# Slots in two rooms, fixed PSUM bank pairs and a first block split ahead, in a kernel of attention and two expert layers

## The chip, the cores and the metric

The kernel runs on one core of a Trainium2 chip. The metric is the device time of one execution in microseconds (us); smaller is better. Work is done by the engines PE (TensorE, matrix products), ACT (ScalarE), DVE (VectorE) and POOL (GpSimd); SP (SyncE) issues nearly all DMA transfers. A step of an engine waits on semaphores for what it needs, and each engine, SP too, works through its own list in order. SBUF is the on-chip memory, PSUM the banks that PE writes its sums into.

## The reference, cut to what matters

```python
def _attn_ref(q, k, v):                         # each 8 x 8 x 576 x 64
    q_s = np.exp(q - np.max(q, axis=-1, keepdims=True))
    q_s = q_s / (np.sum(q_s, axis=-1, keepdims=True) + 1e-09)
    k_s = np.exp(k - np.max(k, axis=2, keepdims=True))
    k_s = k_s / (np.sum(k_s, axis=2, keepdims=True) + 1e-09)
    kv = np.einsum('bhsd,bhse->bhde', k_s, v)
    return np.einsum('bhsd,bhde->bhse', q_s, kv)

def _moe_ref(x, w_in, w_out):                   # x 4608 x 512, w_in 512 x 2048, w_out 2048 x 512
    h = x @ w_in
    return (h * (1.0 / (1.0 + np.exp(-1.702 * h)))) @ w_out

def _moe2_ref(x, w_in, w_out):                  # the same sizes
    h = x @ w_in
    g = np.where(h >= 1, h, np.where(h <= -1, 0.0, (h + 1) ** 2 / 4.0))
    return g @ w_out
```

The output is `_moe2_ref` of `_moe_ref` of the attention's tokens, 4608 x 512 in fp32. The weights come as 64-bit floats and are converted on the chip.

## The kernel before, in words

There are four large products, one after the other, and each is a stage of the program:

1. The **first stage** is attention and the first GEMM (L403 to L405), in nine token blocks of 512 (blocks 0 to 8). A block has 16 column groups `m`, worked off in eight pairs. A pair fills a two-bank PSUM tile `hps` (two such tiles), ACT takes its sigmoid into a tile `sg` (L411, three buffers), DVE multiplies (L412), and SP stores the result as `g0_<block>_<pair>` in DRAM (L413). Attention's work for block j stands in the steps of block j-1, so the last block, 8, has nothing beside its own GEMM. The tokens of a block lie in `xh` and `xl`, two sets that take turns.
2. **pass_out(0)** (gemm L637) multiplies by the first w_out.
3. **pass_in** (gemm L754) multiplies by the second w_in and applies the piecewise function (`finish`, L772 to L774, with the store L777 of `g1`).
4. **pass_out(1)** is pass_out again, with the second w_out, and with the outputs transposed on PE (`turn`).

Every fp32 operand is split in two: ACT copies it rounded to `hi` (L103), DVE subtracts to get `lo` (L104), and each product is three: hi·hi, lo·hi and hi·lo. The last three stages also replace eight block products by seven, in the order PROD = 1, 7, 6, 2, 5, 4, 3 over the quadrants "11", "12", "22" and "21" of a token block, with sums of tiles on DVE (`tt`, L107). There are five token blocks. In a pass_out, a **step** is one (block, p, i) with i from 0 to 3: 12 matmuls that need one split tile. Steps 0 to 3 are p = 1, steps 4 to 7 are p = 7, and so on. Step s is split three steps ahead (LA = 3), into slots that are taken in rotation from R_AT: hi and lo of step s are entries 2s and 2s+1.

**Slots.** After the first stage, its SBUF pools are closed and 27 slots `s0` to `s26` of 4 KB per partition are opened. s0 to s15 hold the loaded tiles (G_AT), and s16 and up are shared out by R_AT (splits of a pass_out), O_AT (its results), E_AT (results of pass_in) and W_AT (conversion of weights in pass_in). Waits between users of a slot go tile by tile.

**PSUM** pools are opened and closed by stage: `hps` and attention's, then z and zx of each pass. `widen` (L535) issues matmuls whose sums nobody uses, two at the head of each pass_out and four at the head of pass_in.

**Order.** The program is laid down in Python order, and a scheduler may move an instruction of an engine ahead of others. SP's DMAs use eight semaphores DMAHW0 to DMAHW7 in turn, so each waits for the one eight before it. The loads of pass_out(0)'s first block stand behind the last `g0` store, at L572 (`Quadrants.load`). Those of pass_out(1)'s first block stand as hooks in the last group of pass_in, at L566.

Of the kernel before, what the change touches and what calls it, by code (L numbers as in the profile page):

```python
# [8 lines left out]
FP32 = mybir.dt.float32  # L9
# [9 lines left out]
def kernel(  # L19
# [11 lines left out]
    nc = tc.nc  # L31
# [27 lines left out]
    half = const.tile([P, 96], FP32, name="half")[:, :1]  # L59

# [124 lines left out]

    with ExitStack() as st0:
        vpool = st0.enter_context(tc.tile_pool(name="va", bufs=1))
        kpool = st0.enter_context(tc.tile_pool(name="k", bufs=3))
        kfpool = st0.enter_context(tc.tile_pool(name="kf", bufs=4))
        qpool = st0.enter_context(tc.tile_pool(name="q", bufs=4))  # L190
        qtpool = st0.enter_context(tc.tile_pool(name="qt", bufs=1))
        sm1 = st0.enter_context(tc.tile_pool(name="sm1", bufs=1))
        sm = st0.enter_context(tc.tile_pool(name="sm", bufs=2))
        xpool = st0.enter_context(tc.tile_pool(name="x", bufs=1))
        sgp = st0.enter_context(tc.tile_pool(name="sg", bufs=3))
        ps_h = st0.enter_context(tc.tile_pool(name="ps_h", bufs=2, space=bass.MemoryType.PSUM))
# [197 lines left out]
        def gemm1(s):  # L394
            j, m = divmod(s, NM)
            xh, xl = x_sb[j]
            if m % 2 == 0:
                h_ps[0] = ps_h.tile([P, 2, TB], FP32, tag="h", name="hps")
# [60 lines left out]
        first_w = {}  # L459
        for p in PROD[:3]:  # L460
            at(NM + 8 * 12 + 1, load_weight, first_w, "out1", p)
# [53 lines left out]
    def operand(bq, p, i):
        b11, b12, b21, b22 = (bq[qd][i] if qd in bq else None for qd in ("11", "12", "21", "22"))
        if p == 7:
            tt(b12, b22, b12, ALU.subtract)
        elif p == 6:
            tt(b11, b12, b11, ALU.add)  # L520
        elif p == 5:
            tt(b12, b22, b11, ALU.subtract)
        return {1: b11, 7: b12, 6: b11, 2: b21, 5: b12, 4: b21, 3: b22}[p]


    def last_sum(bq, i):
        tt(bq["21"][i], bq["11"][i], bq["21"][i], ALU.subtract)

    def widen(pool, w, n):
        for _ in range(n):
            z = pool.tile([P, 2, TB], FP32, tag="zx", name="zx")
            for b in range(2):
                nc.tensor.matmul(  # L535
                    out=z[:, b, :], lhsT=w[:, 0, 0, :P], rhs=w[:, 0, 0, :], start=True, stop=True,
                    skip_group_check=True,
                )


    slots = ctx.enter_context(tc.tile_pool(name="s", bufs=1, reuse_waits="tile"))

    def slot(i, dt=FP32):
        return slots.tile([P, 2, TB], dt, tag=f"s{i}", name=f"s{i}")

    G_AT = {"11": 0, "12": 4, "22": 8, "21": 12}
    R_AT = (24, 25, 26, 19, 18, 17, 16)
    O_AT = {"s7": 20, "u2": 21, "c11": 22}
    C_AT = {p: 4 + 2 * i for i, p in enumerate(PROD)}
    E_AT = (18, 19, 20, 21, 22)  # L550
    W_AT = (23, 24, 25, 26)
    for i in range(27):
        slot(i)

    class Quadrants:
        def __init__(self, ph):
            self.ph, self.t = ph, {}

        def load(self, j, qd, pieces=range(4)):
            n, t0 = HALVES[j], STARTS[j]  # L560
            kh, th = int(qd[0]) - 1, int(qd[1]) - 1
            tiles = self.t.setdefault(j, {}).setdefault(qd, {})
            for i in pieces:
                t = slot(G_AT[qd] + i)
                if self.ph:
                    nc.sync.dma_start(out=t[:, :, :n], in_=g1_dram[j, kh, th, i])  # L566
                else:
                    done = 0
                    while done < n:
                        jb, s = divmod(t0 + th * n + done, TB)  # L570
                        m = min(n - done, TB - s)
                        nc.sync.dma_start(  # L572
                            out=t[:, :, done:done + m], in_=g0_dram[jb][kh * 4 + i][:, :, s:s + m]
                        )
# [307 lines left out]
```

## Time and profile before

| | before |
|---|---|
| median of 3 runs | 1651.31 us (1650.13 to 1653.53) |
| profiled execution | 1651.63 us |
| its span | 1649.9 us |
| mean granted PE clock | 0.984 |
| first stage | 0 to 537 us |
| pass_out(0) | 537 to 900 us |
| pass_in | 900 to 1252.7 us |
| pass_out(1) | 1252.7 to 1650 us |

Times count from the span's start. In a list of an engine's work, a row gives start, length, line and operation with the tile written, an arrow and the tiles read; "x24" is a run of 24 alike, and the bracket is the idle time ahead of it and what ended it. "PEclk" is the clock that PE was granted, as a part of its full speed. A seam, below, is the time in which one stage ends and the next begins.

### The profile page before, as it was taken

To read this page: it belongs to the slowest core of one execution; us is meant where nothing else is said; L and a number is where in the kernel's file an instruction comes from. 1 tells how busy PE (TensorE), PEld (TensorE's weight loads), DVE (VectorE), ACT (ScalarE), POOL (GpSimd) and SP (SyncE) were. 2 spreads that over 40 slices of the span, in tenths; PEclk is the share of its full clock that TensorE was granted. 3 is DMA by queue.
4 is the path that set the end of the run, shared out by engine and by line. 5 is a ranking of instruction groups with operands and counts; after the bars stand their busy time and mean duration, and the time that the engine had idled before them with its cause. 6 is when DMAs were issued, how large, how long until landed. Compare 5 with 4: busy or idle time off the path is not lost. (4 is left out here: it accounts for less than half of the span.)

```text
span 1649.9 us, 20721 instructions
## 1 busy us (share of the span) xinstructions
PE 1579.0 (96%) x7592; PEld 1349.2 (82%) x7592; DVE 1153.9 (70%) x1519; ACT 947.2 (57%) x1135; POOL 8.1 (0%) x45
## 2 busy tenths in 40 slices
PE   5899999999999699999999999999996899999998
PEld 3678888888878588888999887788995688888998
DVE  6999788788732568686776787876545667676673
ACT  4867776776741344444445787877664344444553
POOL 0000000000000000000000000000000000000000
PEclk9999999999999899999999999999998899999999
DMA  7778788788847661715369766664349562524421
GB/s 213 206 238 272 264 261 264 264 276 271 279 164 254 268 193 63 229 46 172 112 207 337 268 236 244 241 230 157 117 145 377 239 203 70 186 68 137 128 77 39
DMA packets 218869, 330.61 MB, mean 200 GB/s; under 512 B 90128, under 2 KB 162832, under 8 KB 216080
## 3 DMA queue, kind: packets, MB, share of 16 engines
q1 hardware_dynamic: 218768, 329.30, 58.9%
q8 instruction: 59, 0.97, 0.2%
q14 instruction: 42, 0.34, 0.1%
HBM read 190.84 MB, written 138.41 MB: 200 GB/s over the span
## 5 line engine op out<-in xcount | busy, mean ns | idle before, releaser
L103 ACT ACTIVATE s<-s 128x1024 fp32r<-128x1024 f32 (+2 forms) x363 | 326.1, 901 | 420.4 <-PE z L637 187.0
L104 DVE TENSOR_TENSOR s<-s,s 128x1024 fp32r<-128x1024 f32 (+2 forms) x363 | 369.9, 1024 | 213.1 <-PE z L637 89.9
L637 PE MATMUL z<-s,w 128*128 128x512 f32 (+1 forms) x1920 | 410.0, 372 | 28.1 <-ACT s L103 26.4
L637 PEld LDWEIGHTS z<-s,w 128*128 128x128 f32 x1920 | 353.7, 190 | 77.0 <-ACT s L103 27.7
L637 PE MATMUL zx<-s,w 128*128 128x512 f32 (+1 forms) x1440 | 303.5, 368 | 1.1 <-ACT s L103 1.1
L637 PEld LDWEIGHTS zx<-s,w 128*128 128x128 f32 x1440 | 261.7, 188 | 34.7 <-ACT s L103 1.5
L403 PE MATMUL hps<-xh,w 128*128 128x512 f32 x576 | 238.5, 414 | 5.2 <-ACT w L103 4.7
L405 PE MATMUL hps<-xh,w 128*128 128x512 f32 x576 | 227.2, 394 | 1.1 <-DVE w L104 1.1
L404 PE MATMUL hps<-xl,w 128*128 128x512 f32 x576 | 226.7, 394 | 0.0
L107 DVE TENSOR_TENSOR s<-s,s 128x1024 f32<-128x1024 f32 (+2 forms) x196 | 205.8, 1059 | 26.6 <-DMA s<-g 19.8
L754 PE MATMUL z<-s,w 128*128 128x512 f32 (+1 forms) x960 | 207.1, 367 | 0.0
L754 PEld LDWEIGHTS z<-s,w 128*128 128x128 f32 x960 | 175.1, 188 | 22.5
L754 PE MATMUL zx<-s,w 128*128 128x512 f32 (+1 forms) x720 | 159.4, 370 | 4.8 <-ACT zx L786 3.5
L754 PEld LDWEIGHTS zx<-s,w 128*128 128x128 f32 x720 | 130.4, 188 | 26.1 <-ACT zx L786 6.8
L412 DVE TENSOR_TENSOR sg<-hps,sg 128x1024 f32<-128x1024 f32 x72 | 87.7, 1217 | 72.7 <-ACT sg L411 72.6
L403 PEld LDWEIGHTS hps<-xh,w 128*128 128x128 f32 x576 | 109.1, 189 | 32.0 <-ACT w L103 5.6
L405 PEld LDWEIGHTS hps<-xh,w 128*128 128x128 f32 x576 | 108.7, 189 | 26.3 <-DVE w L104 2.2
L404 PEld LDWEIGHTS hps<-xl,w 128*128 128x128 f32 x576 | 109.0, 189 | 21.7 <-issue 1.1
L411 ACT ACTIVATE sg<-hps 128x1024 f32<-128x1024 f32 x72 | 73.9, 1027 | 87.9 <-PE hps L405 87.5
L773 ACT ACTIVATE s<-s 128x1024 f32<-128x1024 f32 (+1 forms) x80 | 77.3, 969 | 1.3
L774 DVE SCALAR_TENSOR_TENSOR s<-z,s 128x1024 f32<-128x1024 f32 (+1 forms) x20 | 22.3, 1116 | 55.9 <-ACT s L773 55.7
L774 DVE SCALAR_TENSOR_TENSOR s<-s,s 128x1024 f32<-128x1024 f32 (+1 forms) x40 | 44.7, 1116 | 14.5 <-ACT s L773 12.4
(76 smaller groups left out, 1268.6 us busy)
## 6 DMA issues: line engine op xcount, KB each, us to landing
s<-g SPq DMA_DIRECT2D x96, 512.0 KB, 4.2
g<-sg SPq DMA_DIRECT2D x72, 512.0 KB, 3.1
w<-wp_out SPq DMA_DIRECT2D x14, 2048.0 KB, 10.5
g<-s SPq DMA_DIRECT2D x48, 512.0 KB, 2.9
s<-g SPq DMA_DIRECT2D x48, 384.0 KB, 3.6
wp_out<-w SPq DMA_DIRECT2D x28, 512.0 KB, 4.3
wp_in<-w SPq DMA_DIRECT2D x28, 512.0 KB, 3.9
w<-wp_in SPq DMA_DIRECT2D x7, 2048.0 KB, 8.5
```

The source lines that it names most:

```text
L103: nc.scalar.activation(out=hi, in_=src, func=ACTF.Copy)
L104: nc.vector.tensor_tensor(out=lo, in0=src, in1=hi.bitcast(FP32), op=ALU.subtract)
L107: nc.vector.tensor_tensor(out=o, in0=x, in1=y, op=op)
L403: nc.tensor.matmul(out=hps, lhsT=wh, rhs=xh[:, kk, :], start=(kk == 0), stop=False)
L404: nc.tensor.matmul(out=hps, lhsT=wh, rhs=xl[:, kk, :], start=False, stop=False)
L405: nc.tensor.matmul(out=hps, lhsT=wl, rhs=xh[:, kk, :], start=False, stop=(kk == KD - 1))
L411: nc.scalar.activation(out=sg, in_=hps, func=ACTF.Sigmoid, scale=1.702)
L412: nc.vector.tensor_tensor(out=sg, in0=hps, in1=sg, op=ALU.mult)
L637: nc.tensor.matmul(out=z[:, m, :n], lhsT=a, rhs=b[:, c, :], start=(p in OPENS and i == 0 and c == 0 and x == 0), stop=(i == 3 and c == 1 a ...
L754: nc.tensor.matmul(out=z[:, m, :n], lhsT=a, rhs=b[:, c, :], start=(p in OPENS and c == 0 and x == 0), stop=(c == 1 and x == 2), skip_group ...
L773: nc.scalar.activation(out=t, in_=t, func=ACTF.Square)
L774: nc.vector.scalar_tensor_tensor(out=t, in0=h, scalar=1.0, in1=t, op0=ALU.max, op1=ALU.min)
```

## The change

**Rooms.** The slots become two rooms. s0 to s19 (`NH = 20`) are opened at the start of the first stage's last block, over the attention's pools and the odd blocks' token tiles, which are idle by then. s20 to s26 are opened after the stage, over the even blocks' token tiles and `sg`. PSUM becomes four fixed bank pairs: pairs 0 and 1 are `hps` and later the z of p = 1 and p = 7 in every stage, pair 2 the transposes and pair 3 zx, with pass_in's zx on 3 and 2 in turn.

**Loads and weights.** All 16 loads of pass_out(0)'s first block (now L259) stand at the start of block 8, and the weights 2, 5, 4 and 3 of the first w_out (L184) at four steps within it.

**First tiles.** Steps 0 and 1 of each pass_out are split before the stage begins: in the last steps of block 8, and as hooks in pass_in's last group.

**Tables.** R_AT, E_AT, W_AT and one entry of C_AT name other slots. `widen` is called twice at the end of the first stage (four matmuls) and nowhere else. Lines move: split L103, L104 to L104, L105; tt L107 to L108; the GEMM of a pass_out L637 to L318; the sigmoid L411 to L740, its product L412 to L741, its store L413 to L742.

```diff
-    def widen(pool, w, n):
-        for _ in range(n):
-            z = pool.tile([P, 2, TB], FP32, tag="zx", name="zx")
-            for b in range(2):
+    def widen(i, w):
+        z = bank(i, "zx")
+        for b in range(2):
...
-    slots = ctx.enter_context(tc.tile_pool(name="s", bufs=1, reuse_waits="tile"))
+    NH = 20
+    def open_room(key, side, tags, shape):
+        pool = ctx.enter_context(tc.tile_pool(
+            name=key, bufs=1, side=side, reuse_waits="tile",
+            **({"space": bass.MemoryType.PSUM} if key.startswith("p") else {})
+        ))
+        for i in tags:
+            rooms[key[0], i] = pool
+            pool.tile(shape, FP32, tag=f"{key[0]}{i}", name=f"{key[0]}{i}")
...
-    R_AT = (24, 25, 26, 19, 18, 17, 16)
+    R_AT = (16, 17, 18, 19, 24, 25, 26)
+    C_AT[PROD[-1]] = 20
-    E_AT = (18, 19, 20, 21, 22)
-    W_AT = (23, 24, 25, 26)
+    E_AT = (22, 23, 24, 25, 26)
+    W_AT = (16, 17, 18, 19)
...
-            widen(zxpool, sl[1], 1)
-            LA = 3
-            for s in range(LA):
-                ready(s)
+        def run(hooks, done):
+            for s in range(done, LA):
+                ready(s)
...
-            widen(zxpool, sl[1], 2)
...
+        for i, p in enumerate(PROD[3:]):
+            at((NB - 1) * NM + 4 * i + 3, load_weight, w_out1, "out1", p)
+        for i in range(2):
+            at(NB * NM - 3 + i, ready0, i)
...
         for s in range(NB * NM):
+            if s == (NB - 1) * NM:
+                st1.close()
+                open_room("s0", "left", range(NH), [P, 2, TB])
+                open_room("p1", "left", (2, 3), [P, 2, TB])
+                for qd in ("11", "12", "22", "21"):
+                    g0.load(0, qd)
             gemm1(s)
...
-    for what in ("11", "12", "22", 2, "21", 5, 4, 3):
-        if isinstance(what, str):
-            g0.load(0, what)
-        else:
-            load_weight(w_out1, "out1", what)
+        widen(3, w_out1[1])
+        widen(2, w_out1[1])
+    open_room("s1", "right", range(NH, 27), [P, 2, TB])
...
-    pass_out(0, g0, w_out1, hooks)
+    run0(hooks, 2)
...
-        1: [(g1.load, (0, "11")), lw(1), (g1.load, (0, "12", (0, 1)))],
+        1: [lw(1), (g1.load, (0, "12", (0, 1)))],
         7: [lw(7), (g1.load, (0, "12", (2, 3)))],
-        6: [(g1.load, (0, "22", (0, 1)))],
-        2: [(g1.load, (0, "22", (2, 3))), lw(6)],
+        6: [(g1.load, (0, "22", (0, 1))), (ready1, (0,))],
+        2: [(g1.load, (0, "22", (2, 3))), lw(6), (ready1, (1,))],
...
+                if g == 1 and p == 1:
+                    g1.load(0, "11")
...
-    pass_out(1, g1, w_out2, {})
+    run1({}, 2)
```

Three places show what this does to the order. The first is **SP in the first stage's last block and behind it**, with the semaphores that each DMA waits for; `g0_8_0` is the first store of block 8. Before:

```order
L413 DMA g0_7_7_149<-sg_4405 128x1024 [waits DMAHW2_49,DVE_49]
L413 DMA g0_8_0_150<-sg_4434 128x1024 [waits DMAHW3_49,DVE_49]
L183 DMA w_4706<-wp_out1_2_68 128x4096 [waits DMAHW4_49,PE_49]
L413 DMA g0_8_1_151<-sg_4463 128x1024 [waits DMAHW5_49,DVE_49]
...
L413 DMA g0_8_7_157<-sg_4637 128x1024 [waits DMAHW6_49,DVE_49]
L572 DMA s0_4682<-g0_0_0_86 128x1024 [waits DMAHW7_49]
L572 DMA s1_4684<-g0_0_1_87 128x1024 [waits DMAHW0_49]
```

In the changed kernel, the same place reads:

```order
L742 DMA g0_7_6_152<-sg_4372 128x1024 [waits DMAHW1_49,DVE_49]
L259 DMA s0_4454<-g0_0_0_90 128x1024 [waits DMAHW2_49,PE_49,Activation_49]
L259 DMA s1_4456<-g0_0_1_91 128x1024 [waits DMAHW3_49]
L742 DMA g0_7_7_153<-sg_4413 128x1024 [waits DMAHW4_49,DVE_49]
L259 DMA s2_4458<-g0_0_2_92 128x1024 [waits DMAHW5_49]
...
L259 DMA s15_4484<-g0_0_7_97 128x1024 [waits DMAHW2_49]
L742 DMA g0_8_0_154<-sg_4511 128x1024 [waits DMAHW3_49,DVE_49]
L742 DMA g0_8_1_155<-sg_4540 128x1024 [waits DMAHW4_49,DVE_49]
L184 DMA w_4544<-wp_out1_2_72 128x4096 [waits DMAHW5_49,PE_49]
```

The 16 loads have moved from behind the last store of block 8 to ahead of its first.

The second place is **ACT at the end of the first stage**, where it makes the hi tiles of pass_out(0)'s first steps; s0 to s7 are the tiles of steps 0 to 7 (0 to 3 of p = 1; s4 to s7 of p = 7). Before:

```order
L103 ACTIVATE s24_4731<-s0_4682 128x1024 [waits DMAHW7_49]
L103 ACTIVATE s26_4735<-s1_4684 128x1024 [waits DMAHW0_49]
L103 ACTIVATE s18_4739<-s2_4686 128x1024 [waits DMAHW1_49,Activation_49]
L103 ACTIVATE s16_4756<-s3_4688 128x1024 [waits DMAHW2_49]
L103 ACTIVATE s25_4773<-s4_4690 128x1024 [waits DVE_49,PE_49]
```

In the changed kernel, from the start of block 8 on (L740 is the sigmoid of a pair):

```order
L104 ACTIVATE s16_4695<-s0_4454 128x1024 [waits DMAHW2_49,DVE_49]
L104 ACTIVATE s18_4712<-s1_4456 128x1024 [waits DMAHW3_49]
L740 ACTIVATE sg_4511<-hps_4486 128x1024 [waits DMAHW0_49,DVE_49,PE_49]
...
L740 ACTIVATE sg_4728<-hps_4699 128x1024 [waits DMAHW1_49,DVE_49,PE_49]
L104 ACTIVATE s17_4786<-s4_4462 128x1024 [waits PE_49]
L104 ACTIVATE s19_4803<-s5_4464 128x1024 [waits PE_49]
L104 ACTIVATE s18_4857<-s0_4454 128x1024 [waits DVE_49,PE_49]
L104 ACTIVATE s24_4752<-s2_4458 128x1024 [waits DMAHW5_49]
L104 ACTIVATE s26_4769<-s3_4460 128x1024
```

The hi tiles of steps 0 and 1 have moved ahead of all sigmoids of block 8, and those of steps 4, 5 and 8 (s0 read a second time) stand ahead of step 2's. DVE's lo tiles follow the same order, and PE takes the steps as 0, 1, 4, 2, 3, 5, 6, 7, 8.

The third place is **ACT where pass_in ends and pass_out(1) begins**. Before (L772 and L773 belong to the last `finish` of pass_in):

```order
L772 ACTIVATE s18_10112<-zx_9976,half_64 128x2x384 [waits DVE_49]
L773 ACTIVATE s18_10112<-s18_10112 128x2x384 [waits Activation_49]
L103 ACTIVATE s25_10176<-s4_9988 128x1024 [waits DVE_49,PE_49]
L103 ACTIVATE s19_10193<-s5_9990 128x1024 [waits DVE_49,PE_49]
L103 ACTIVATE s26_10247<-s0_9978 128x1024 [waits PE_49]
L103 ACTIVATE s18_10142<-s2_9982 128x1024 [waits DMAHW1_49]
L103 ACTIVATE s17_10212<-s6_10009 128x1024 [waits DVE_49,PE_49]
```

In the changed kernel:

```order
L104 ACTIVATE s17_10164<-s4_9987 128x1024 [waits DVE_49,PE_49]
L104 ACTIVATE s24_10130<-s2_9739 128x1024 [waits DMAHW6_49]
L104 ACTIVATE s19_10181<-s5_9989 128x1024 [waits DVE_49,PE_49]
L104 ACTIVATE s18_10235<-s0_9735 128x1024 [waits PE_49]
L104 ACTIVATE s26_10147<-s3_9741 128x1024 [waits DMAHW5_49]
L104 ACTIVATE s25_10200<-s6_10008 128x1024 [waits DMAHW2_49,DVE_49,PE_49]
```

Step 2's hi has moved from slot 18, written by the last `finish`, to slot 24, and stands earlier; step 3's now goes to slot 26, and its wait is the store of an earlier `finish`.

## Rows read from the trace of the kernel before

**Rows 1.** The page's busy times by engine, and PE's tenths in 40 slices.
```profile
PE 1579.0 (96%) x7592; PEld 1349.2 (82%) x7592; DVE 1153.9 (70%) x1519; ACT 947.2 (57%) x1135; POOL 8.1 (0%) x45
...
PE   5899999999999699999999999999996899999998
```

**Rows 2.** Windows by stage: last block, then eight steps after each seam.
```profile
core 0: us, PE busy (x) PEld busy (x) DVE busy (x) ACT busy (x) POOL busy (x), PEclk, DMA share, GB/s
493.30:536.80 43.50, 43.50 (x194) 36.02 (x193) 9.79 (x8) 8.23 (x8) 0.00 (x0) 1.00 0.68 242
536.80:575.10 38.30, 25.08 (x100) 19.55 (x99) 22.37 (x19) 13.25 (x13) 0.00 (x0) 0.82 0.74 288
1252.60:1302.30 49.70, 28.75 (x100) 21.95 (x99) 26.80 (x24) 13.01 (x15) 0.00 (x0) 0.76 0.93 387
```

**Rows 3.** Timeline of SP's issues at the first seam (start, length, line).
```profile
539.29 0.32 SPq L413 DMA_DIRECT2D g<-sg  x1
539.67 17.32 SPq L572 DMA_DIRECT2D s<-g  x16
```

**Rows 4.** Timeline of PE at the first seam.
```profile
549.09 0.80 PE L637 MATMUL z<-s,w 128*128 128x512 f32 x1 [11.69 <-ACT s L103]
```

**Rows 5.** Timeline of ACT at the first and the last seam.
```profile
547.98 1.06 ACT L103 ACTIVATE s<-s 128x1024 fp32r<-128x1024 f32 x1 [9.97 <-DMA s<-g]
...
1284.74 1.06 ACT L103 ACTIVATE s<-s 128x1024 fp32r<-128x1024 f32 x1 [12.14 <-DMA g<-s]
```

**Rows 6.** Timeline of DVE at the last seam: a subtraction, six sums.
```profile
1264.10 1.23 DVE L104 TENSOR_TENSOR s<-s,s 128x1024 fp32r<-128x1024 f32 x1 [6.43 <-PE z L637]
...
1268.79 6.89 DVE L107 TENSOR_TENSOR s<-s,s 128x1024 f32<-128x1024 f32 x6
```

**Rows 7.** The page's DMA issues: KB each, median us from issue to landing.
```profile
s<-g SPq DMA_DIRECT2D x96, 512.0 KB, 4.2
g<-sg SPq DMA_DIRECT2D x72, 512.0 KB, 3.1
```

**Rows 8.** Windows early in the first stage, columns as in rows 2.
```profile
80.00:83.00 3.00, 1.21 (x4) 0.73 (x5) 3.00 (x7) 2.96 (x8) 0.00 (x0) 0.99 0.71 223
83.00:86.40 3.40, 3.40 (x10) 2.66 (x9) 3.40 (x8) 1.67 (x3) 0.00 (x0) 0.51 0.87 279
```

**Rows 9.** Timelines of DVE and ACT in block 8: third product, fourth sigmoid.
```profile
510.85 1.23 DVE L412 TENSOR_TENSOR sg<-hps,sg 128x1024 f32<-128x1024 f32 x1 [4.22 <-ACT sg L411]
...
515.23 1.03 ACT L411 ACTIVATE sg<-hps 128x1024 f32<-128x1024 f32 x1 [4.41 <-PE hps L405]
```

**Rows 10.** SP's store as pass_out(0) ends, and its time to land.
```profile
900.12 0.52 SPq L649 DMA_DIRECT2D x<-s  x1
...
x<-s SPq DMA_DIRECT2D x1, 384.0 KB, 8.5
```

**Rows 11.** Timeline of PE as pass_out(1) begins.
```profile
1257.73 1.22 PE L535 MATMUL zx<-w 128*128 128x512 f32 x2 [5.00 <-DVE s L774]
1258.75 8.08 PE L637 MATMUL z<-s,w 128*128 128x512 f32 x24
...
1285.84 0.80 PE L637 MATMUL z<-s,w 128*128 128x512 f32 x1 [13.88 <-ACT s L103]
```

**Rows 12.** Timeline of SP as pass_in ends: two loads, three of four stores.
```profile
1245.31 5.24 SPq L566 DMA_DIRECT2D s<-g  x2
...
1259.87 0.52 SPq L777 DMA_DIRECT2D g<-s  x1
...
1263.62 0.52 SPq L777 DMA_DIRECT2D g<-s  x1
...
1271.96 0.52 SPq L777 DMA_DIRECT2D g<-s  x1
```

**Rows 13.** Landing times: those stores (1251 to 1272.5), the load of 1245.31.
```profile
g<-s SPq DMA_DIRECT2D x4, 384.0 KB, 12.9
...
s<-g SPq DMA_DIRECT2D x1, 512.0 KB, 17.0
```

More of the change, by code (lines that the diff above doesn't have):

```diff
@@ L59 @@
     half = const.tile([P, 96], FP32, name="half")[:, :1]
+    ctx.enter_context(tc.tile_pool(name="even", bufs=1, side="right")).tile([P, 120], FP32, name="even")
     PROD = (1, 7, 6, 2, 5, 4, 3)
@@ new lines, in slot, with bank, __init__, load @@
+    def slot(i, dt=FP32):
+        return rooms["s", i].tile([P, 2, TB], dt, tag=f"s{i}", name=f"s{i}")
+    def bank(i, name="z"):
+        return rooms["p", i].tile([P, 2, TB], FP32, tag=f"p{i}", name=name)
+    G_AT = {"11": 0, "12": 4, "22": 8, "21": 12}
+    R_AT = (16, 17, 18, 19, 24, 25, 26)
+    O_AT = {"s7": 20, "u2": 21, "c11": 22}
+    C_AT = {p: 4 + 2 * i for i, p in enumerate(PROD)}
+    C_AT[PROD[-1]] = 20
+    E_AT = (22, 23, 24, 25, 26)
+    W_AT = (16, 17, 18, 19)
+    class Quadrants:
+        def __init__(self, ph):
+            self.ph, self.t = ph, {}
+        def load(self, j, qd, pieces=range(4)):
+            n, t0 = HALVES[j], STARTS[j]
+            kh, th = int(qd[0]) - 1, int(qd[1]) - 1
+            tiles = self.t.setdefault(j, {}).setdefault(qd, {})
+            for i in pieces:
+                t = slot(G_AT[qd] + i)
+                if self.ph:
+                    nc.sync.dma_start(out=t[:, :, :n], in_=g1_dram[j, kh, th, i])
+                else:
+                    done = 0
+                    while done < n:
+                        jb, s = divmod(t0 + th * n + done, TB)
+                        m = min(n - done, TB - s)
+                        nc.sync.dma_start(
+                            out=t[:, :, done:done + m], in_=g0_dram[jb][kh * 4 + i][:, :, s:s + m]
+                        )
+                        done += m
+                tiles[i] = t[:, :, :n]
@@ new lines, with __init__, load, ready @@
+    class Tokens:
+        def __init__(self):
+            self.t, self.ops = {}, {}
+        def load(self, j):
+            n = HALVES[j]
+            for i, qd in enumerate(("11", "12", "22", "21")):
+                t = slot(i)[:, :, :n]
+                nc.sync.dma_start(out=t, in_=x1_dram[j, int(qd[0]) - 1, int(qd[1]) - 1])
+                self.t.setdefault(j, {})[qd] = [t]
+        def ready(self, j, p):
+            n = HALVES[j]
+            src = operand(self.t[j], p, 0)
+            hi, lo = (slot(C_AT[p] + i, FP32R)[:, :, :n] for i in range(2))
+            split(hi, lo, src)
+            self.ops[j, p] = hi, lo
+            if p == 2:
+                last_sum(self.t[j], 0)
@@ L397, in gemm1 @@
             if m % 2 == 0:
-                h_ps[0] = ps_h.tile([P, 2, TB], FP32, tag="h", name="hps")
+                h_ps[0] = bank(m // 2 % 2, "hps")
             hps = h_ps[0][:, m % 2, :]
```

503 lines of the change are left out of this document (228 added, 275 removed).

## The prediction, made before the changed kernel ran

> **What bounds the kernel now.** Read the busy times first: TensorE (PE) is busy 1579 us of a span of 1649.9 [rows 1], so what an edit can win is PE's 71 us of idle time and its slow stretches. The line of PE's share in 40 slices of 41 us shows where [rows 1]: in the 1st, in the 14th, where the first GEMM ends and pass_out(0) begins, and in the 31st and 32nd, where pass_in ends and pass_out(1) begins. The windows by stage give those two seams a size. In the last block of the first stage 192 matmuls take 43.50 us at a clock of 1.00 [rows 2], so a matmul of 512 columns has a pitch of 43.50/192 = 0.227 us, and a step of 12 takes 2.72. The first eight steps of a pass (96 matmuls) would take 21.8 us. They take 38.3 after the first stage and 49.7 after pass_in, with mean granted clocks of 0.82 and 0.76 [rows 2]. The seams thus hold 16.5 + 27.9 = 44.4 us of loss, and the diff works on these.
>
> **The first seam.** Before, SP issues the 16 tile loads only from 539.67 on, behind the last g0 store [rows 3]. PE has done its two widening matmuls by then and stands for 11.69 us until 549.09 [rows 4]; ACT, which makes its hi, has waited 9.97 for a load [rows 5]. [...] In the new program the loads stand in the last block, and steps 0 and 1 are split there. Step 0 follows the stage's last matmul. Four widening matmuls stand within that block (before, two stood behind it), 0.9 us more, so step 0 starts at 536.8 + 0.9 = 537.7.
>
> Eight steps then take 21.8, plus bubbles that I read from the new order. PE goes from steps 0 and 1 to step 4, whose lo goes into the slot of step 1's hi: a DVE subtraction of 1.23 [rows 6] less the one matmul (0.23) that needs no lo, 1.0. Next ACT makes the hi of step 8 ahead of that of step 2, into a slot that step 4 reads: two copies of 1.06 [rows 5] less two matmuls, 1.7. Then step 2's lo, 1.0 again. Step 2's hi also waits for the last g0 store: issued at 539.29 [rows 3], 3.1 to land [rows 7], so 542.4, 4 us ahead of its turn at about 547. Step 8 starts at 537.7 + 21.8 + 3.7 = 563.2 and not at 575.1: 11.9 gained. Gaps of this kind have a precedent: between 80 and 83 PE worked 1.21 of 3 us, and in the next 3.4 its clock was 0.51 [rows 8]. One such stretch costs 1.7, so I take **10.2**. [...]
>
> **The last block** pays for it. 16 loads (8.4 MB) now stand ahead of the store g0_8_0 on SP. There are three sg buffers, so the sigmoid of the fourth pair waits for that store; behind it on ACT stand the next sigmoids, and PE waits for the bank pair that they free. The nearest rate: 387 GB/s at a DMA share of 0.93 [rows 2], so 416 at full share, 1.26 us for a load. The first can be issued as the block starts (493.3) and lands 4.2 later [rows 7], the 16th at 497.5 + 15 × 1.26 plus 1.26 for a store between them, 517.7, and g0_8_0 at about 519. Sigmoid and product, 1.03 + 1.23 [rows 9], end at 521.3. PE wants that bank pair for the sixth pair at 493.3 + 5 × 5.44 + 0.9 = 521.4. DVE has six subtractions and sums more in front of that product, 6 × 1.15 [rows 6] from 512.1 (the third product, 510.85 + 1.23 [rows 9]) to 519.0: hidden as well. This is an edge without margin; I take **−0.3**, bounds 0 and −3.
>
> [...]
>
> **Between pass_out(0) and pass_in** four widening matmuls go: **0.9**. W_AT and E_AT move s7 to slot 23, whose store is issued at 900.12 and takes 8.5 [rows 10]. The copy thus comes at 908.6 to 909.7, and the product that needs it is the sixth of the pass, due near 900 + 5 × 2.72 = 913.6: nothing.
>
> **The second seam.** SP's order is the same before and after, so the loads come when they came. Before, PE idles 5.00 until 1257.73, since the widening takes a bank pair whose reader ends late; it then does 24 matmuls in 8.08 (0.34 each, most at half clock), and stands 13.88 at the hi of step 2 [rows 11]. ACT waited 12.14 for that [rows 5], because its slot 18 is the source of the store issued at 1271.96 [rows 12], 12.9 to land [rows 13]. Behind it, in order, stood the hi of steps 6 and 7.
>
> After, in four parts:
> 1. Steps 0 and 1 are split by the time pass_in ends: they run from 1252.7 to 1258.1.
> 2. Step 4 needs the load issued at 1245.31 [rows 12], 17.0 to land [rows 13]: 1262.3. A subtraction, a copy and a subtraction (1.15 + 1.06 + 1.23) give 1265.8; its 12 matmuls end by 1271 at half clock.
> 3. Step 2's hi now goes to slot 24, free early. Its lo goes to slot 25, source of the store of 1259.87, landed at 1272.8: lo at 1274.0. Step 3's hi waits for the store of 1263.62, so 1276.5, with its lo at 1278.8 [rows 12, 13].
> 4. Step 3 ends at 1281.3 to 1282.5, and 35 matmuls of steps 5 to 7 take 7.9: 1289.2 to 1290.4 with some half clock. Step 8 starts at 1290.5 and not at 1302.3: **11.8**. Bounds: 13.1 with full clock throughout, 6 if both stores land 6 us later than the median.
>
> The wait has moved from the fourth store to the third; what is late next is step 3's slot.
>
> **Sum.** 10.2 + 0.9 + 11.8 − 0.3 = 22.6. The profiled execution took 1651.63, 0.3 from the median of 1651.31: 1651.6 − 22.6 = **1629**. Its own range, 1625 to 1633.
>
> **Rivals.**
> - *The bubbles vanish and the clock holds.* Seam one gives 13.5, seam two 13.1: 1651.6 − 27.2 = 1624. For it: PE works through until 543 with no gap. Against it: the waits above are in the order.
> [...]
> - *The second seam is paced by its transfers.* The DMA share there is 0.93 [rows 2]. If what the third store waits for slips as the loads do, only the 5.00 of the widening and its 0.5 go: 10.2 + 0.9 + 5.5 − 0.3 = 16.3, so 1635. Against it: PE waited for a slot there, not for a tile.
> - *The last block stops* (slower). SP, ACT and DVE each work in order; ACT waits for a load to split step 0, and all sigmoids of the block stand behind it. Each 1 us by which a load takes more than 1.26 moves the stores by 17. The other gains are used up once that costs 22.9, at 2.6 us a load. If loads went one at a time, 4.2 each [rows 7], it would cost 17 × 2.9 = 50: 1679. Against it: 16 loads before were issued within 17.32 [rows 3], 1.08 each. [...]
> - *No change:* the change doesn't do what it says, because a room waits for all of its predecessor; the first loads would then come at the stage's end, and what one seam gains the last block pays: 1651.
>
> **How the numbers follow.** Forecast 0.56, high clock 0.14, low clock 0.13, transfers 0.10, no change 0.03, slower 0.04. Faster by more than 0.2% (3.3 us, about what a measurement of this kernel tells from nothing) is 0.56 + 0.14 + 0.13 + 0.10 = 0.93. The range takes in 1624, 1635 and 1636 with 2 to 3 us about them: 1621 to 1638.
>
> **What would show it.** Right: the first pass_out matmul within 1 us of the last hps one and no idle over 2 us among the next 96; 96 matmuls in about 25.5 us; PE idle under 1 us in the last block; after pass_in 24 matmuls at once, then about 6 us of idle behind a load, and 3 and 2 before steps 2 and 3. Wrong: ACT idle on a g store in the last block, half clock over more than 5 us after the first seam, or step 2's hi still waiting for a store.

## The result and the profile after

The changed kernel takes 1629.12 us (median of 4 runs, 1627.00 to 1630.73) where the kernel before takes 1651.83: a ratio of 0.9862, 95% interval 0.9845 to 0.9879. Run again later, beside other runs of before, it took 1627.54 against 1648.98, a ratio of 0.9872 (0.9855 to 0.9888). So 21.4 to 22.7 us were won where 22.6 were forecast. The profiled execution took 1628.26, its span 1626.5. The page after, with the two lines that answer to [rows 1]:

```profile
span 1626.5 us, 20715 instructions
...
PE 1573.0 (97%) x7588; PEld 1345.8 (83%) x7588; DVE 1154.4 (71%) x1519; ACT 946.9 (58%) x1135; POOL 8.1 (0%) x45
...
PE   5899999999999999999999999999998999999998
```

The 6 of the 14th slice is now a 9, and the 6 and 8 of the 31st and 32nd are an 8 and a 9. The windows by stage, columns as in [rows 2], for block 8 and for the first 96 matmuls after each seam:

```profile
489.90:535.98 46.08, 44.81 (x199) 36.76 (x197) 18.87 (x16) 10.12 (x10) 0.00 (x0) 1.00 0.98 389
535.98:565.05 29.07, 25.50 (x97) 19.92 (x96) 17.75 (x15) 11.29 (x12) 0.00 (x0) 0.88 0.32 124
...
1242.10:1278.90 36.80, 26.02 (x98) 19.73 (x97) 25.62 (x23) 13.14 (x15) 0.00 (x0) 0.86 1.02 425
```

The first seam went from 38.30 to 29.07 us, the last from 49.70 to 36.80. PE's longest waits there (answering to [rows 4] and [rows 11]):

```profile
519.52 0.50 PE L732 MATMUL hps<-xh,w 128*128 128x512 f32 x1 [1.27 <-DVE sg L741]
...
542.97 0.50 PE L318 MATMUL z<-s,w 128*128 128x512 f32 x1 [1.16 <-DVE s L105]
...
547.63 0.49 PE L318 MATMUL z<-s,w 128*128 128x512 f32 x1 [1.64 <-ACT s L104]
...
548.89 0.80 PE L318 MATMUL z<-s,w 128*128 128x512 f32 x1 [0.77 <-DVE s L105]
...
1254.25 0.80 PE L318 MATMUL z<-s,w 128*128 128x512 f32 x1 [6.49 <-ACT s L104]
...
1263.80 0.50 PE L318 MATMUL z<-s,w 128*128 128x512 f32 x1 [3.82 <-DVE s L105]
```

The longest wait is now 1.64 at the first seam, where it was 11.69, and 6.49 at the last, where it was 13.88. The 6.49 is another wait than the 13.88: PE waits for step 4 there, and its wait for step 2 is the 3.82. Cut at the same matmuls, the two profiled executions compare like this (us, by the starts of PE's matmuls; the end of a stage is put 0.23, one pitch, behind the start of its last matmul):

| stretch | before | after | difference |
|---|---|---|---|
| start to block 8 | 493.27 | 489.98 | -3.29 |
| block 8 | 43.52 | 45.99 | +2.47 |
| first 96 matmuls of pass_out(0) | 38.30 | 29.07 | -9.23 |
| rest of pass_out(0) | 323.23 | 323.23 | 0.00 |
| pass_in | 354.31 | 353.89 | -0.41 |
| first 96 matmuls of pass_out(1) | 49.68 | 36.73 | -12.95 |
| rest, to the span's end | 347.55 | 347.55 | 0.00 |

The total came out as forecast, but its parts did not all do so: the first line was not in the sum at all, and the second and third together gave 6.75 and not 9.9.

### The profile page after: what moved, and what is told of

It is laid out like the page before. It is cut to its first block, busy times and chain, and to the rows that moved or that the text cites. A ratio compares the mean times of both kernels' runs of the same rounds, so it can differ in the third digit from the quotient of the medians.

```text
span 1626.5 us, 20715 instructions
## 1 busy us (share of the span) xinstructions
PE 1573.0 (97%) x7588; PEld 1345.8 (83%) x7588; DVE 1154.4 (71%) x1519; ACT 946.9 (58%) x1135; POOL 8.1 (0%) x45
## 5 line engine op out<-in xcount | busy, mean ns | idle before, releaser
L104 ACT ACTIVATE s<-s 128x1024 fp32r<-128x1024 f32 (+2 forms) x363 | 325.8, 901 | 404.2 <-PE z L318 204.3
L105 DVE TENSOR_TENSOR s<-s,s 128x1024 fp32r<-128x1024 f32 (+2 forms) x363 | 369.9, 1025 | 199.6 <-PE z L318 84.0
L318 PE MATMUL z<-s,w 128*128 128x512 f32 (+1 forms) x1920 | 409.5, 372 | 14.3 <-ACT s L104 8.1
L318 PEld LDWEIGHTS z<-s,w 128*128 128x128 f32 x1920 | 352.7, 190 | 63.4 <-ACT s L104 9.0
L318 PE MATMUL zx<-s,w 128*128 128x512 f32 (+1 forms) x1440 | 303.2, 368 | 0.0
L318 PEld LDWEIGHTS zx<-s,w 128*128 128x128 f32 x1440 | 261.7, 188 | 33.3
L108 DVE TENSOR_TENSOR s<-s,s 128x1024 f32<-128x1024 f32 (+2 forms) x196 | 205.6, 1060 | 28.8 <-DMA s<-g 21.8
L432 PEld LDWEIGHTS z<-s,w 128*128 128x128 f32 x960 | 175.0, 188 | 22.5
L741 DVE TENSOR_TENSOR sg<-hps,sg 128x1024 f32<-128x1024 f32 x72 | 87.7, 1219 | 63.8 <-ACT sg L740 63.6
L733 PEld LDWEIGHTS hps<-xl,w 128*128 128x128 f32 x576 | 108.9, 189 | 21.3 <-issue 1.1
L740 ACT ACTIVATE sg<-hps 128x1024 f32<-128x1024 f32 x72 | 73.8, 1026 | 86.1 <-PE hps L734 71.6
```

The costliest lines, as they stand in the source:

```text
L104: nc.scalar.activation(out=hi, in_=src, func=ACTF.Copy)
L105: nc.vector.tensor_tensor(out=lo, in0=src, in1=hi.bitcast(FP32), op=ALU.subtract)
L108: nc.vector.tensor_tensor(out=o, in0=x, in1=y, op=op)
L318: nc.tensor.matmul(out=z[:, m, :n], lhsT=a, rhs=b[:, c, :], start=(p in OPENS and i == 0 and c == 0 and x == 0), stop=(i == 3 and c == 1 a ...
L432: nc.tensor.matmul(out=z[:, m, :n], lhsT=a, rhs=b[:, c, :], start=(p in OPENS and c == 0 and x == 0), stop=(c == 1 and x == 2), skip_group ...
L733: nc.tensor.matmul(out=hps, lhsT=wh, rhs=xl[:, kk, :], start=False, stop=False)
```

## The experiments

All of them in one table: lengths of the three stretches in the profiled execution, the median and the ratio to before with its interval. "96 of out" are the first 96 matmuls of a pass_out, from the end of the stage ahead of it. Each ratio is to runs of before that were taken beside the kernel; their medians were 1651.83, 1651.25, 1650.26 and 1648.98.

| kernel | block 8 | 96 of out(0) | 96 of out(1) | median | ratio |
|---|---|---|---|---|---|
| before | 43.5 | 38.3 | 49.7 | | 1 |
| after | 46.0 | 29.1 | 36.7 | 1629.12 | 0.9862 (0.9845 to 0.9879) |
| after again | 45.8 | 27.7 | 36.5 | 1627.54 | 0.9872 (0.9855 to 0.9888) |
| old slots at the last seam | 48.3 | 27.8 | 49.2 | 1641.97 | 0.9942 (0.9921 to 0.9964) |
| before, no widening | 43.5 | 40.0 | 50.6 | 1649.58 | 0.9998 (0.9980 to 1.0015) |
| loads written last | 43.5 | 30.3 | 36.5 | 1628.28 | 0.9860 (0.9837 to 0.9882) |
| tokens under the room | 43.5 | 42.4 | 36.7 | 1637.74 | 0.9925 (0.9908 to 0.9942) |
| free slots | 46.1 | 29.1 | 27.9 | 1620.03 | 0.9814 (0.9793 to 0.9835) |
| + paired loads | 45.8 | 27.6 | 28.6 | 1615.19 | 0.9788 (0.9772 to 0.9804) |
| + eight slots | 45.8 | 23.1 | 27.0 | 1613.48 | 0.9778 (0.9759 to 0.9796) |
| + later quadrant 21 | 44.4 | 28.2 | 28.4 | 1616.78 | 0.9800 (0.9782 to 0.9818) |
| + order by hand | 44.4 | 21.8 | 26.2 | 1607.67 | 0.9752 (0.9737 to 0.9766) |
| + later sums | 44.4 | 22.2 | 23.9 | 1606.44 | 0.9745 (0.9731 to 0.9760) |

One part of the change has no run of its own: the hooks that split steps 0 and 1 ahead. The run with the old slots, which comes next, leaves them out as well. In its trace PE, ACT and DVE run the same operations in the same order as in the changed kernel through block 8 and the first 150 us of pass_out(0), with the same three waits at the seam (1.16, 1.64 and 0.76), and step 0 of both passes starts right behind the stage ahead of it. So the scheduler puts those splits there by itself as soon as the slots allow it. With the new tables at the last seam this was not run.

### What the last seam's gain is: the slot tables

The changed kernel with the tables of before in pass_in and pass_out(1):

```diff
-    R_AT = (16, 17, 18, 19, 24, 25, 26)
+    R_ATS = ((16, 17, 18, 19, 24, 25, 26), (24, 25, 26, 19, 18, 17, 16))
...
-    C_AT[PROD[-1]] = 20
-    E_AT = (22, 23, 24, 25, 26)
-    W_AT = (16, 17, 18, 19)
+    E_AT = (18, 19, 20, 21, 22)
+    W_AT = (23, 24, 25, 26)
...
-    run0(hooks, 2)
+    run0(hooks, 0)
...
-    run1({}, 2)
+    run1({}, 0)
```

> The changed kernel, but pass_in and pass_out(1) use the slot tables of the kernel before (pass_out(0) keeps the new ones), and nothing is split early in the code (which moves no instruction). Theory (the last store of pass_in sets the seam, whatever stands ahead of it): step 2's hi waits for that store again, about 13 us of idle ahead of step 2, and step 8 starts 49 us after pass_in's last matmul where the changed kernel needs 36.8: about 1641. Rival (the 5 us of idle ahead of the widening were on the path): step 8 at 44 us, about 1636. Rival (the tables do nothing): 1629.

Measured: 1641.97, with 49.2 us at the last seam. PE's timeline, then ACT's, of this run ahead of step 2:

```profile
1277.70 0.79 PE L317 MATMUL z<-s,w 128*128 128x512 f32 x1 [15.31 <-ACT s L104]
```

```profile
1276.59 1.06 ACT L104 ACTIVATE s<-s 128x1024 fp32r<-128x1024 f32 x1 [13.56 <-DMA g<-s]
```

The idle time of [rows 11] is back, and longer: step 0 began at once, without the widening, step 1 after 3.09 us of idle time within it, and the time won ahead of step 2 was waited out there. So 12.4 of the 12.95 us won at the last seam come from the tables, and the wait that came back tells by which entry: in the changed kernel step 2's slot no longer is the source of pass_in's last store. The same from the other side, with the kernel before and its widening taken out:

```diff
-            widen(zxpool, sl[1], 1)
-            widen(zxpool, sl[1], 2)
```

> The kernel before without its eight widening matmuls. Theory (both seams are set by loads and stores, so what is saved ahead of them is lost in a longer wait): only the four matmuls ahead of pass_in count, 0.9 us, so about 1650.7, with PE's idle time of 5.0 at the last seam gone and the one ahead of step 2 grown from 13.9 to some 19. Rival (the wait of the widening was on the path): 0.9 + 5.5 less, about 1645.4. For the start of the program, where the changed kernel's first GEMM began 2.5 us earlier: 39.8 us if that belongs to the change, between 37 and 40 if it is chance.

This kernel's results change with the eight matmuls gone (see the last section), so it serves for the time of the rest alone. Measured: 1649.58, no change that can be told from none (0.9998, and the interval reaches from 3.3 us less to 2.5 more, so the rival's 6.4 less is out). PE's timeline:

```profile
1262.80 0.80 PE L637 MATMUL z<-s,w 128*128 128x512 f32 x1 [5.17 <-ACT s L103]
...
1283.93 0.80 PE L637 MATMUL z<-s,w 128*128 128x512 f32 x1 [15.47 <-ACT s L103]
```

The 5.00 ahead of the widening [rows 11] came back as 5.17 ahead of step 4, where 0.84 had stood, and 1.6 more ahead of step 2. An idle time that reads 5 us in the trace was worth nothing that these runs can show.

### What the first seam's gain is: the loads' early start

The first attempt to delay the loads was to write them behind the last block:

```diff
...
-                for qd in ("11", "12", "22", "21"):
-                    g0.load(0, qd)
             gemm1(s)
...
+        for qd in ("11", "12", "22", "21"):
+            g0.load(0, qd)
         widen(3, w_out1[1])
...
-    run0(hooks, 2)
+    run0(hooks, 0)
```

> The changed kernel, but the 16 tile loads of pass_out(0) stand behind the last block, and steps 0 and 1 of that pass are split there. Theory (the loads are the whole gain of the first seam): PE idles about 11 us there again, the first 96 matmuls take some 38 us and not 29.1, and the 1.3 us of idle in block 8 are gone: about 1637. Rival (half clock takes most of the gain at this seam whatever is loaded): within 3 us of 1629. Start of the first GEMM: 37.3 us if the early start belongs to the change.

Measured: 1628.28, no loss. It didn't test what it was to test. The order shows that the scheduler hoisted the loads all the same: five stand ahead of the first store of block 8 and three more among the rest. The other eight come behind it. It does show that eight loads spread over the block cost it nothing (43.5 us), with 30.3 us at the seam, 0.9 of them the widening, which stands behind the block here: eight early loads do as well as sixteen. What allows a load to go early is where its slot lies, not its place in the code. So the next run moved the memory:

```diff
-                (x1pool if j % 2 else x0pool).tile([P, KD, TB], FP32R, tag="xh", name="xh"),
-                (x1pool if j % 2 else x0pool).tile([P, KD, TB], FP32R, tag="xl", name="xl"),
+                (x0pool if j % 2 else x1pool).tile([P, KD, TB], FP32R, tag="xh", name="xh"),
+                (x0pool if j % 2 else x1pool).tile([P, KD, TB], FP32R, tag="xl", name="xl"),
```

> The changed kernel, with the two token sets exchanged: block 8's tokens lie where the left room opens, so the tile loads can start only when the block's last matmul has read them (the order shows them behind the seventh store). Theory (the loads' early start is the gain at the first seam, and the store behind 16 loads the idle time in block 8): block 8 takes 44.4 us with no idle, PE then stands 8 to 10 us, and the first 96 matmuls take 36 to 40 us and not 29.1: about 1636. Rival (bank pairs and the missing widening at the head of the pass carry that gain): 31 us or less, about 1630.

Measured: 1637.74. The windows of block 8 and of the 96 matmuls after it, and SP's timeline:

```profile
492.05:535.60 43.55, 43.55 (x194) 36.06 (x193) 9.80 (x8) 8.23 (x8) 0.00 (x0) 1.00 0.68 241
535.60:577.93 42.33, 31.31 (x102) 23.26 (x100) 26.93 (x23) 13.39 (x14) 0.00 (x0) 0.80 0.66 261
```

```profile
535.80 14.53 SPq L259 DMA_DIRECT2D s<-g  x16
```

With the loads behind the block, block 8 has no idle time and the seam is back at 42.3 us, even above the 38.3 of [rows 2] (0.9 of it the widening, which stands behind the block here too). The bank pairs, the missing widening at the head of the pass and the tables were all still there, so at the first seam the early loads are the gain. The seam came out longer than the 36 to 40 us expected; PE's waits in it are 11.0 us together, and the granted clock is 0.80.

### What is left there: ACT's order, slots and one store

The three waits of the first seam and the idle time of block 8 were then taken away in steps. Each kernel below contains the ones ahead of it. First a table of its own for pass_out(1), so that steps 2 and 3 use slots that no late store reads:

```diff
-    R_AT = (16, 17, 18, 19, 24, 25, 26)
-    O_AT = {"s7": 20, "u2": 21, "c11": 22}
+    R_ATS = ((16, 17, 18, 19, 24, 25, 26), (16, 17, 18, 19, 20, 21, 24))
+    O_ATS = ({"s7": 20, "u2": 21, "c11": 22, "c12": 23}, {"s7": 25, "u2": 26, "c11": 22, "c12": 25})
...
```

> The changed kernel, with a slot table of its own for pass_out(1): steps 2 and 3 use slots 20, 21 and 24 (two free when pass_in's last product ends, one with an early store) and not 24, 25, 26; the pass's results go to 25 and 26. Theory (the second wait at the last seam is for stores that read the slots): steps 0, 1 and 2 run at once, PE idles some 4 us until step 4's tile, nothing ahead of steps 2 and 3, and step 8 starts about 30 us after pass_in where the changed kernel has 36.8: about 1622.5. Rival (transfers pace the seam, and the next tile or weight is late in their place): step 8 at 35 us or later, 1627 or more.

Measured: 1620.03, and 27.9 us at the last seam where 30 were expected: with less idle time the clock was also higher, 0.94 where it was 0.86. One wait stayed, 3.22 us for step 4's hi. The window of the seam and that wait:

```profile
1240.85:1268.75 27.90, 23.92 (x97) 18.96 (x96) 21.37 (x20) 12.75 (x15) 0.00 (x0) 0.94 1.03 423
```

```profile
1252.36 0.50 PE L318 MATMUL z<-s,w 128*128 128x512 f32 x1 [3.22 <-ACT s L104]
```

Step 4 needs the sum of two tiles, so the next edit loads the second of them earlier, ahead of the weight:

```diff
-    G_AT = {"11": 0, "12": 4, "22": 8, "21": 12}
+    G_AT = {"11": (0, 1, 2, 3), "12": (4, 6, 8, 10), "22": (5, 7, 9, 11), "21": (12, 13, 14, 15)}
...
-        1: [lw(1), (g1.load, (0, "12", (0, 1)))],
-        7: [lw(7), (g1.load, (0, "12", (2, 3)))],
+        1: [lw(1), (g1.load, (0, "12", (0,))), (g1.load, (0, "22", (0,)))],
+        7: [(g1.load, (0, "12", (1,))), (g1.load, (0, "22", (1,))), lw(7)],
...
```

> The slot table of the run with free slots (1620), and the tiles of quadrants 12 and 22 for pass_out(1)'s first block are loaded in pairs, two of each ahead of the weight of p = 7. Theory (what is left at the last seam is the wait for step 4's second tile, 3.2 us, and for its subtraction): that tile now lands some 7 us earlier, the weight 2.5 us later but before step 2 ends, so the first 96 matmuls take 23 to 24 us and not 27.9: about 1615.5. Rival (the transfers as a whole are the limit, so another tile is late by as much): 27 to 28 us, 1620.

The median fell to 1615.19, but the seam didn't get shorter: 28.6 us, somewhat above the rival's 27 to 28. The wait of 3.22 was gone, and five shorter ones had come in its place, 3.8 us together, the longest of them (1.90) on DVE and only 0.38 on a transfer, that of the weight. So the seam stayed long, but not because another tile was late, as the rival has it. In the profiled execution, block 8 to the end of the first seam took 73.4 us where the run ahead of it took 75.1; there the edit only gives the tiles of two quadrants other slots. The fall of the median can't be put down to this edit, and the intervals of the two ratios overlap. The windows of the two seams in this run:

```profile
535.77:563.39 27.62, 24.05 (x97) 18.92 (x96) 17.75 (x15) 11.29 (x12) 0.00 (x0) 0.94 0.34 133
1239.30:1267.91 28.61, 24.81 (x97) 18.82 (x96) 25.31 (x23) 12.64 (x15) 0.00 (x0) 0.94 1.03 425
```

Next, eight slots in rotation in pass_out(0), where the result c12 moves from slot 23 to 20 to make room:

```diff
-    R_ATS = ((16, 17, 18, 19, 24, 25, 26), (16, 17, 18, 19, 20, 21, 24))
+    R_ATS = ((16, 17, 18, 19, 24, 25, 26, 23), (16, 17, 18, 19, 20, 21, 24))
-    O_ATS = ({"s7": 20, "u2": 21, "c11": 22, "c12": 23}, {"s7": 25, "u2": 26, "c11": 22, "c12": 25})
+    O_ATS = ({"s7": 20, "u2": 21, "c11": 22, "c12": 20}, {"s7": 25, "u2": 26, "c11": 22, "c12": 25})
...
```

> The kernel with the paired loads, and pass_out(0)'s splits rotate over eight slots, not seven, so step 4 takes both slots of step 0 and step 8's hi stands behind step 4 alone. Theory (the three waits of 1.2, 1.6 and 0.8 us at the first seam are slots and ACT's order, and the half clock behind them follows from them): those waits go, the granted clock stays at 1.00 through the seam, and the first 96 matmuls take 22.5 to 23.5 us and not 29.1: 6 us less than the paired loads alone, about 1609.5. Rival (the low clock belongs to the seam, not to the waits): 25 to 27 us, 1612 to 1613.

Measured: 1613.48, and 23.1 us at the first seam, as expected. The window of that seam in this run:

```profile
535.61:558.71 23.10, 22.49 (x97) 17.78 (x96) 18.98 (x16) 11.15 (x11) 0.00 (x0) 1.00 0.40 157
```

The granted clock is 1.00 through the seam, where it was 0.94 with the paired loads and 0.88 in the changed kernel, and the waits are down from 3.57 us to one of 0.61. The half clock at this seam came with the waits, and went with them. The median missed the expected 1609.5 and fell by less than the 4.5 us of this profile (1.7; the intervals overlap). The four executions lie at 1610.4, 1611.0, 1616.0 and 1616.0, with a mean clock of 0.997 in the first two and 0.995 in the others; the profile is of the one at 1611.0, so what the seam took in the longer ones isn't shown. Then the store of block 8:

```diff
-                for qd in ("11", "12", "22", "21"):
+                for qd in ("11", "12", "22"):
                     g0.load(0, qd)
+            if s == (NB - 1) * NM + 4:
+                g0.load(0, "21")
```

> The kernel with eight slots, and the four loads of quadrant 21 stand behind the first two stores of block 8. Theory (the 1.3 us of idle in block 8 are the wait for the store g0_8_0 behind 16 loads): with 12 loads ahead of it that idle time is gone, block 8 takes 44.4 us and not 45.7 to 46. But in this order the hi of step 9 also stands ahead of step 2's, so PE waits about 2.7 us after step 5, and the seam takes some 26 us: about 1.7 us more in all than with eight slots alone. Rival (the idle time in block 8 is DVE's six sums, not the store): block 8 stays at 45.7 us or more.

Measured: 1616.78. ACT's timeline of this run in block 8 and PE's at the seam:

```profile
515.32 1.03 ACT L739 ACTIVATE sg<-hps 128x1024 f32<-128x1024 f32 x1 [4.54 <-DMA g<-sg]
```

```profile
550.79 0.59 PE L318 MATMUL z<-s,w 128*128 128x512 f32 x1 [2.09 <-ACT s L104]
```

The fourth sigmoid comes 22.1 us into the block, where it came 27.2 us into it (517.18 - 489.98), and block 8 takes 44.4 us: its idle time was the store. The wait that the new ACT order makes was there too (2.09 and 0.86), but the granted clock was 0.88 over the seam, where it was 1.00 with eight slots, so the seam took 28.2 and not 26, and the median rose by 3.3 where 1.7 were expected:

```profile
537.66:565.90 28.24, 25.29 (x98) 19.77 (x96) 19.00 (x16) 11.26 (x11) 0.00 (x0) 0.88 0.37 140
```

Both at once, with the order set by hand; `behind(a, b)` is a small helper of this kernel that keeps the scheduler from moving a ahead of b:

```diff
...
-            split(hi, lo, src)
+            made[s] = split(hi, lo, src)
+            if s in (8, 9):
+                behind(made[s][0], made[3][0])
```

> The kernel with the later loads of quadrant 21 (12 loads ahead of the store g0_8_0), with one order given by hand: the hi of steps 8 and 9 stand behind that of step 3 on ACT. Theory (both costs of the first seam, the idle time in block 8 and ACT's order, can be had away together): block 8 takes 44.4 us, the first 96 matmuls of pass_out(0) 22.5 to 23.5 us, the last seam 27 as with eight slots: about 1612. Rival (the half clock at the first seam comes without those waits): 26 us or more there, 1615.

Measured: 1607.67. The windows of block 8 and of both seams:

```profile
490.01:534.44 44.43, 44.43 (x197) 36.79 (x196) 18.87 (x16) 10.24 (x10) 0.00 (x0) 1.00 0.99 396
534.44:556.20 21.76, 21.76 (x97) 18.02 (x96) 18.44 (x16) 11.16 (x11) 0.00 (x0) 1.00 0.50 181
1231.24:1257.40 26.16, 23.23 (x98) 17.65 (x96) 24.91 (x23) 12.62 (x15) 0.00 (x0) 1.00 1.03 424
```

The first seam is now at 21.8, what 96 matmuls take at full clock (96 x 0.227, the pitch at a clock of 1.00 in [rows 2]), and nothing is left there. The median is 4 us below the expected 1612, and the two seams account for some 2 of them (21.8 where 22.5 to 23.5 were expected, 26.2 where 27 were). At the last one DVE is busy 24.9 of 26.2 us. The last edit moves the four sums of p = 5 behind the lo of step 7:

```diff
...
-            tt(b12, b22, b11, ALU.subtract)
+            ins = tt(b12, b22, b11, ALU.subtract)
+            if after:
+                behind(ins, after[1])
...
```

> The kernel with the order given by hand, and the four sums of p = 5 in the first block of each pass_out stand behind the lo of step 7 on DVE. Theory (with the stores and the second tile out of the way, DVE bounds the last seam: it is busy 25.7 of 27.7 us there with sums that nothing needs yet, ahead of the lo tiles that PE waits for): 4.9 us of DVE's work move behind, and the first 96 matmuls of pass_out(1) take 23.5 to 25 us and not 27: about 1609.5. Rival (transfers bound it now, at a DMA share of 1.02 to 1.08): 26.5 us or more, 1612.

Measured: 1606.44, with this window at the last seam:

```profile
1232.89:1256.76 23.87, 22.55 (x97) 17.74 (x96) 22.89 (x21) 12.51 (x15) 0.00 (x0) 1.00 1.02 422
```

26.2 became 23.9 us at the same DMA share, so the order of DVE's work bounded the seam and the transfers didn't. The four kernels ahead of this one, with the same tables and loads at the last seam, took 26.2 to 28.6 us there in their profiles, so 23.9 lies below all of them. In the medians the step is 1.2 us and the intervals overlap. This kernel beats both: 0.9745 of before, 21 to 23 us below the changed kernel.

### What belongs to chance

> The changed kernel once more, for the parts of the program that the change doesn't touch. Theory (the 3.3 us by which its first stage ended its eighth block earlier are chance: ten profiles began the first GEMM anywhere from 36.8 to 40.7 us, with the same order of instructions): the first GEMM begins somewhere in that band, block 8 takes 45.8 to 48.3 us, the two seams 28 to 30 and 36 to 37 us, as before, and the time is 1629 within 2 us. Rival (the new pools start the program sooner): 37.3 us again and never above 38.

Measured: the first GEMM began at 38.30 us (37.27 in the first profile of the same program), at 40.66 in the run with the old slots and at 40.73 in the one with the loads written last. So the rival is out. Block 8 and the last seam fell into the expected bands, and the first seam (27.7) just below its own. Other stretches vary as well. From the first GEMM to block 8 the thirteen profiles took 451.9 to 453.5 us, and for pass_in, which few of these edits touch, 351.6 to 354.3. A step of one or two us between two medians of the table is therefore no proof of an edit; what an edit does is read at the seam that it touches.

## Why the prediction was right, point by point

**The last seam** went as worked out, nearly step by step. Counted from pass_in's end: step 4's hi was to come at 11.8 us, and PE went on with it at 12.1; step 2's lo was to come at 21.3, and PE went on with it at 21.6; step 3's hi was to start at 23.8. The waits behind the first and the last of those moments are ACT's, the load's sum first, then the store of slot 26:

```profile
1253.14 2.02 ACT L104 ACTIVATE s<-s 128x1024 fp32r<-128x1024 f32 x2 [8.22 <-DVE s L108]
...
1265.92 1.06 ACT L104 ACTIVATE s<-s 128x1024 fp32r<-128x1024 f32 x1 [5.31 <-DMA g<-s]
```

That is 1265.92 - 1242.17 = 23.75. The 2 us of idle time that were to stand ahead of step 3 didn't come: step 2 ran in part at half clock (a granted clock of 0.67 from 1263.8 to 1267.3, and 0.50 in every window of 0.5 us from 1265.0 to 1268.0) and took up that time. Step 8 came 36.7 us after pass_in and not 37.8, since step 3 ended at 28.6, the early end of what was worked out, and steps 5 to 7 ran at full clock: 12.95 gained, within the bounds of 6 and 13.1 about the 11.8. The rival of the transfers, with its 5.5, was wrong. The stores that steps 2 and 3 wait for did not slip: they landed 20.3 and 23.7 us after pass_in's end, where 20.1 and 23.8 had been worked out. And the run without the widening shows that the 5.5 themselves were not on the path of the kernel before. A DMA share of 1.02 doesn't make the DMA the bound: at 1.02 to 1.03 this seam took 36.8, 27.9 and 23.9 us, as slots, the order of the loads and the order of DVE's work were changed.

**The first seam** had the right mechanism and a term too small. The bubbles were 1.16, 1.64 and 0.77, sum 3.57, against 1.0, 1.7 and 1.0. But the half clock lasted 0.12 x 29.07 x 2 = 7.0 us (in windows of 0.5 us the seam has a clock of 0.50 in each from 548.5 to 555.0, 0.68 in the one ahead of them, and 0.99 or 1.00 in all others), a loss of 3.5, where the sum had one stretch of 3.4 us and a loss of 1.7. So the 96 matmuls took 29.1 us, where the sum has 27.2 (21.8 + 3.7 + 1.7) and the list of signs 25.5, and the term of 10.2 measured 8.3 (9.23 less the 0.9 of the widening in block 8). "Half clock over more than 5 us after the first seam" was named as a sign of error, and it came. The second profile of the same program had a clock of 0.94 over 27.7 us, by the same working an estimated 3.3 us at half, which is the stretch that was assumed: the size varies between executions, and one precedent [rows 8] couldn't tell that. The two times forecast on the clock lie on either side of the 1627.0 to 1630.7 measured: 1624, with neither bubbles nor half clock, and 1636, with a low clock. The 1636 was the author's estimate: a clock of 0.82 over 38.3 us [rows 2] costs 6.9 us, 5.2 more than the 1.7 of the one stretch, and 2 more were put on the last seam.

**Block 8** was called an edge without margin, and it went over it: SP and ACT of the changed kernel, answering to [rows 9]:

```profile
492.87 12.95 SPq L259 DMA_DIRECT2D s<-g  x14
506.79 1.57 SPq L742 DMA_DIRECT2D g<-sg  x2
```

```profile
517.18 1.94 ACT L740 ACTIVATE sg<-hps 128x1024 f32<-128x1024 f32 x2 [9.65 <-DMA g<-sg]
```

The sigmoid waited 9.65 us for the store and came 27.2 us into the block, where 25.7 had been worked out. So a second sign of error, ACT idle on a g store in the last block, came too, though the working itself has that wait. PE stood 1.27 us, not 0.3, within the bounds of 0 and 3; the block grew by 2.47 in all, 0.9 of it the widening. In the run with the old slots it was 1.98, and the clock then fell to 0.73 in the 6.4 us behind it, 1.7 us more. The rate was right: the trace has the loads' landings 1.25 us apart. What was too small is the time of the stores among them: the last store of block 7 landed 2.67 us after the load ahead of it, and g0_8_0 1.62 us after the 16th load, where the sum has 1.26 for each. The windows above moved 389 GB/s in block 8, at a DMA share of 0.98, and 425 at the last seam, at 1.02, where the working had 416 at full share.

**Between the passes**, 0.9 was forecast, and the first 96 matmuls of pass_in took 21.80 and not 22.71 us: 0.91. Over the whole of pass_in only 0.41 of it is left in this pair, which is less than that stage varies from run to run.

**The part ahead of block 8**, 3.29 us in the profiled pair, wasn't in the sum and isn't the change's. 2.55 of it lie ahead of the first GEMM, which the programs of after's kind began anywhere from 36.8 to 40.7 us and those of before's kind at 38.8 and 39.8; the other 0.74 lie between there and block 8, a stretch in which before's kind took 453.45 and 451.88 us. In this pair the 3.29 happened to make up for the 3.2 us that block 8 and the first seam fell short: without them the pair shows some 20 us and not 22.6. The medians, over four and more runs, say 21.4 to 22.7, so the sum was not far off, but that the profiled pair agrees with it this closely is luck.

**The rivals on the other side.** One load at a time (1679) was far off: 14 loads were issued within 12.95 us, with eight outstanding at most. And the room did not wait for all of its predecessor (1651), since the first two loads were issued at 490.21, 0.2 us into block 8.

## What to carry to other kernels

An idle time in front of a stage is worth what the next wait behind it leaves: follow each wait to its last releaser and ask what that depends on, since here 5 us ahead of the widening were worth nothing that could be measured and a slot number was worth 12. Memory that comes free early lets a scheduler start loads early by itself; where the load is written matters less than what lies under its tile (1628.28 with the loads written last, 1637.74 with the tokens under the room). When a wait is gone, look for the next engine in the window, even one that was never the bound (DVE, here, in order, with sums that nobody needed yet ahead of those that PE waited for).

## What was not expected of the hardware

The start of the program varies by up to 4.0 us between the profiles, with the same order of instructions on every engine up to the first GEMM. In the traces, the eight `px` matmuls ahead of the first GEMM take 5.4 us before and 3.7 us after; but the kernel before without its widening also has 3.7, and the run with the old slots 5.3, so the length doesn't go with the kernel. The windows show when the clock was low, of before first, of the changed kernel second:

```profile
25.00:30.00 5.00, 2.68 (x15) 2.26 (x16) 4.33 (x13) 3.03 (x6) 0.00 (x0) 0.83 0.93 259
...
35.00:40.00 5.00, 5.00 (x9) 2.19 (x9) 3.41 (x7) 3.05 (x6) 0.00 (x0) 0.66 1.01 277
```

```profile
25.00:30.00 5.00, 3.57 (x17) 3.26 (x18) 3.68 (x11) 3.01 (x6) 0.00 (x0) 0.66 1.09 254
...
35.00:40.00 5.00, 5.00 (x18) 3.03 (x17) 5.00 (x9) 3.64 (x7) 0.00 (x0) 1.00 1.06 277
```

The low stretch falls once on PE's busiest matmuls and once on a stretch with waits. What decides which was not tried.

Without the widening's eight matmuls, whose sums nothing reads, the results of the kernel before change: they lie off the reference's by a relative error of 0.061. What these matmuls do for the later ones is not shown by any run here.
